# A third buffer for the lower words of the weights, and one weight step moved earlier, in a fused attention and SwiGLU kernel

## The chip, the cores and the metric

One core of one Trainium2 chip runs the whole program. The metric is the device time of one execution in microseconds (us), as a median of several runs. An engine here is one of TensorE (PE), VectorE (DVE), ScalarE (ACT) and GpSimd (POOL); SyncE (SP) issues most of the transfers. PEld is the loading of weights into TensorE, which runs beside its matmuls.

## The reference, cut to what matters

```
scores = (q @ k.T) / sqrt(64)                      # 8 batches x 8 heads, 576 x 576
scores = where(scores >= rowmax(scores) - tau, scores, -1e9)
attn   = softmax(scores)                           # over the kept scores
x      = (attn @ v) as (8*576, 8*64)               # 4608 x 512, heads side by side
g, val = x @ w_gate, x @ w_val                     # 512 -> 1536
out    = (g * sigmoid(g) * val) @ w_out            # 1536 -> 512
```

The inputs of the program are float32, but for the weights (`w_gate`, `w_val`, `w_out`), which come as float64. The kernel itself has to make float32 words of them.

## The kernel before, in words

**Segments and slots.** The attention of two heads of one batch is a segment, `i` = 0 to 31. The main loop (from L864) runs over a list of segments `n`, and within each over its tiles of 128 query rows; one turn of the loop is called slot (n, x) here. Tile 4 is the half tile that holds the last 64 rows. Segments n = 0 to 3 are the first part: tiles 0 and 1 of the four head pairs of batch 0. Segments n = 4 to 7 are the second part: tiles 2, 3 and 4 of the same head pairs. So the first tile of the second part is slot (4,0). From n = 8 on ("halved" in the code) a segment has five tiles.

**A slot.** The order on each engine is the order in which the program issues. A slot issues, in this order: the score matmuls (`sc`, L343, L351 or L356) into two tiles of PSUM, which the slot before has to have left; the row maxima on DVE (L378, L366); the product with `v` of an earlier tile (`xa`, L483, and the ACT copy L489); the threshold and the exponential on ACT (`th` L384 or L381, L385); the turning of the tile before it by PE (`tp`, `end`, L455 to L462) and the ACT copies of that (L463, L467, L468); then a weight step's split and fetch; then the masked product and row sum on DVE (L389), the reciprocal (L414), and the scaling by it on ACT (L397) and POOL (L395); then a join; and then `fill`, which issues a share of the matmuls of the feed-forward block (`pg`, `pv`, L545, with the gate's ACT instructions L558 and L559 and the DVE product L565; later `po`). How much each `fill` issues is set by counts when the program is built, not by time. `xa`, `tp`, `end`, `pg`, `pv` and `po` share four PSUM banks in turn.

**Weight steps.** The weights come in 24 steps of 128 x 768 float64 numbers: steps 1 to 16 for `w_gate` and `w_val`, 17 to 24 for `w_out`. A step is

- a fetch (`fetch_weights`, SP, L182 or L185) into one of six places,
- a split (`split_weights`, ACT): L196 writes the upper words' magnitude into the final place of the weights, and L197 writes a correction from the lower words into a buffer `lo`, taken in turn from the list `los` (L157),
- a join (`join_weights`, DVE and POOL): DVE's L203, L207 and L210 make the float32 bits, and POOL's L212 adds the correction out of `lo`. The place is free for another fetch after L210, and the buffer after L212.

Each slot after the first one splits one step, fetches what it can and joins the oldest that was split. `los` has two buffers, so L197 of step p waits for L212 of step p-2. In two slots, (4,2) and (5,2), which have only the half tile (`double`, L897), two steps are joined at once and a further one is split after them:

```
            double = t == NT and NP <= n < NP + 2
            if more and not double:
                join_weights()
            fill(part)
            next(go)
            fill(part)
            if double:
                join_weights(2)
                split_weights()
                fetch_weights(2)
            gates()
```

`need` keeps the matmuls of the block behind the weights that they read. With this, step 7 is joined in slot (4,0), steps 9 and 10 in (4,2), 13 and 14 in (5,2), 21 in (8,0), 22 in (8,1), 23 in (8,2) and 24 in (8,4). The tile `ob` (pool `op`, one buffer) is where finished output rows are put together; the first of them is written at 249.1 us.

## Time and profile before

| | us |
|---|---|
| median of 5 runs | 1510.97 (1510.58 to 1511.27) |
| the profiled execution | 1511.27, of which its span 1509.5 |
| PE busy in the span | 1483.4 (98%) |
| DVE, ACT, POOL busy | 995.8, 726.5, 642.0 |
| granted PE clock, mean over the span | 0.999 |

The 24 weight steps lie between 17 and 184 us. Busy time is what the profile counts; matmuls overlap, so that one 128x256 matmul stands there with 0.38 us, while a row of 16 in the last part of the trace takes 3.45 us. "Idle before" at an instruction is the time for which its engine had nothing to do ahead of it, and the name after the arrow is what ended this wait.

### The profile page before, as it was taken

To read this page: it belongs to the slowest core of one execution; us is meant where nothing else is said; L and a number is where in the kernel's file an instruction comes from. 1 tells how busy PE (TensorE), PEld (TensorE's weight loads), DVE (VectorE), ACT (ScalarE), POOL (GpSimd) and SP (SyncE) were. 2 spreads that over 40 slices of the span, in tenths; PEclk is the share of its full clock that TensorE was granted. 3 is DMA by queue.
4 is the path that set the end of the run, shared out by engine and by line. 5 is a ranking of instruction groups with operands and counts; after the bars stand their busy time and mean duration, and the time that the engine had idled before them with its cause. 6 is when DMAs were issued, how large, how long until landed. Compare 5 with 4: busy or idle time off the path is not lost. (4 is left out here: it accounts for less than half of the span.)

```text
span 1509.5 us, 31512 instructions
## 1 busy us (share of the span) xinstructions
PE 1483.4 (98%) x11808; PEld 1124.7 (75%) x11808; DVE 995.8 (66%) x3040; ACT 726.5 (48%) x2158; POOL 642.0 (43%) x640
## 2 busy tenths in 40 slices
PE   9999799999999999999999999999999999999998
PEld 6777564477777777787777777777777777888887
DVE  7887987777777777747677666677666767412212
ACT  6777665555545545434545445454544554311110
POOL 2554643366453545435444444544545353500000
PEclk9999999999999999999999999999999999999999
DMA  8643311211112111112111011112110120000000
GB/s 183 178 129 112 76 33 40 53 33 33 46 33 47 33 42 23 40 23 46 33 40 20 21 46 33 46 33 47 33 42 13 40 48 16 1 14 1 15 15 15
DMA packets 177064, 66.93 MB, mean 44 GB/s; under 512 B 159888, under 2 KB 159888, under 8 KB 176912
## 3 DMA queue, kind: packets, MB, share of 16 engines
q1 hardware_dynamic: 170880, 56.62, 16.5%
q0 software_dynamic: 2432, 7.87, 1.4%
q8 instruction: 94, 1.54, 0.4%
q10 hardware_dynamic: 3600, 0.43, 0.2%
q14 instruction: 58, 0.48, 0.1%
HBM read 55.44 MB, written 9.44 MB: 43 GB/s over the span
## 5 line engine op out<-in xcount | busy, mean ns | idle before, releaser
L395 POOL TENSOR_SCALAR pall<-pall,ri 128x288 f32<-128x288 f32 (+1 forms) x260 | 265.0, 1029 | 344.3 <-DVE ri L405 315.1
L545 PE MATMUL pv<-xall,wgv 128*128 128x256 f32 x1728 | 404.0, 382 | 2.4 <-ACT pall L463 2.0
L545 PE MATMUL pg<-xall,wgv 128*128 128x256 f32 x1728 | 403.4, 382 | 0.2 <-ACT pall L463 0.2
L545 PEld LDWEIGHTS pv<-xall,wgv 128*128 128x128 f32 x1728 | 323.6, 190 | 67.7 <-issue 21.8
L545 PEld LDWEIGHTS pg<-xall,wgv 128*128 128x128 f32 x1728 | 323.7, 190 | 65.5 <-issue 22.0
L366 DVE TENSOR_REDUCE mx<-sc 128x2 f32<-128x576 f32 x252 | 180.6, 751 | 237.5 <-PE sc L343 236.7
L389 DVE SCALAR_TENSOR_TENSOR pall<-sc,th,pall 128x288 f32<-128x288 f32 (+1 forms) x540 | 258.2, 528 | 31.4 <-ACT pall L385 31.4
L385 ACT ACTIVATE pall<-sc,nm 128x288 f32<-128x288 f32 (+1 forms) x540 | 236.4, 510 | 0.6
L381 ACT ACTIVATE th<-nm,cut 128x4 f32<-128x4 f32 (+1 forms) x140 | 41.6, 297 | 383.6 <-DVE nm L370 383.6
L577 POOL TENSOR_TENSOR ht<-ht,gt 128x512 f32<-128x512 f32 x84 | 107.0, 1273 | 193.7 <-DVE ht L565 109.8
L434 DVE STREAM_TRANSPOSE pall<-pall 128x576 f32<-128x576 f32 x252 | 181.4, 754 | 2.8 <-POOL pall L395 2.8
L643 PE MATMUL po<-wo,ht 128*128 128x256 f32 x768 | 177.5, 381 | 0.0
L343 PE MATMUL sc<-kT,qT 64*32 64x288 f32 x4032 | 157.8, 410 | 12.8 <-DVE pall L389 11.4
L643 PEld LDWEIGHTS po<-wo,ht 128*128 128x128 f32 x768 | 144.6, 190 | 26.4 <-issue 6.0
L565 DVE SCALAR_TENSOR_TENSOR ht<-tn,pv 128x512 f32<-128x512 f32 x102 | 69.9, 685 | 132.3 <-PE pv L545 119.1
L397 ACT ACTIVATE pall<-pall,ri 128x288 f32<-128x288 f32 (+1 forms) x264 | 132.9, 553 | 0.0
L319 ACT COPY sums<-sums 32x4 f32<-32x4 f32 (+1 forms) x560 | 108.4, 194 | 50.0 <-DVE pall L389 38.6
L558 ACT ACTIVATE tn<-pg 128x512 f32<-128x512 f32 x108 | 64.8, 600 | 139.8 <-PE pg L545 133.0
L509 PE MATMUL xa<-pall,vall 64*64 64x288 f32 x2016 | 128.7, 405 | 0.0
L343 PEld LDWEIGHTS sc<-kT,qT 64*32 64x32 f32 x4032 | 58.7, 105 | 90.4 <-issue 61.6
L509 PEld LDWEIGHTS xa<-pall,vall 64*64 64x64 f32 x2016 | 74.3, 133 | 50.7 <-ACT sums L319 3.6
L661 POOL TENSOR_TENSOR ht<-ht,xall 128x256 f32<-128x256 f32 x48 | 34.1, 729 | 156.3 <-PE po L643 155.1
(110 smaller groups left out, 1338.4 us busy)
## 6 DMA issues: line engine op xcount, KB each, us to landing
vall<-in_v_dram SPq DMA_DIRECT2D x112, 144.0 KB, 3.3
kraw<-in_k_dram SPq DMA_DIRECT2D x114, 72.0 KB, 2.8
qraw<-in_q_dram SPq DMA_DIRECT2D x112, 72.0 KB, 2.4
out_dram<-ob POOLq DMA_DIRECT2D x28, 256.0 KB, 2.8
wo<-in_moe_w_gate_dram SPq DMA_DIRECT2D x16, 384.0 KB, 3.6
wo<-in_moe_w_val_dram SPq DMA_DIRECT2D x16, 384.0 KB, 4.1
xall<-in_moe_w_out_dram SPq DMA_DIRECT2D x5, 768.0 KB, 4.7
wo<-in_moe_w_out_dram SPq DMA_DIRECT2D x3, 768.0 KB, 4.8
```

Source lines behind the costliest of these rows:

```text
L319: nc.scalar.copy(out, in_[:, :, 0])
L343: nc.tensor.matmul(ps[g * G:(g + 1) * G, h, 0:SH], qT[hs, col + a * G:col + (a + 1) * G], kT[hs, c * SH:(c + 1) * SH], start=True, stop=True)
L366: nc.vector.tensor_reduce(out=mx[:, 2 * x:2 * x + 2, 0], in_=tile_[:, :, 0:SH], axis=AX.X, op=ALU.max, negate=True)
L385: nc.scalar.activation(ps[x], scs[x], AF.Exp, bias=nm[:, x:x + 1])
L389: nc.vector.scalar_tensor_tensor(out=ps[x], in0=scs[x], scalar=th[:, x:x + 1], in1=ps[x], op0=ALU.is_ge, op1=ALU.mult, accum_out=sm[:, x, ...
L395: nc.gpsimd.tensor_scalar(out=ps[x], in0=ps[x], scalar1=ri[:, x:x + 1], scalar2=None, op0=ALU.mult)
L397: nc.scalar.activation(ps[x], ps[x], AF.Copy, scale=ri[:, x:x + 1])
L434: nc.vector.transpose(out=p, in_=p)
L509: nc.tensor.matmul(xa[a][h * D:(h + 1) * D, at:at + n * G].rearrange("d (i q) -> d i q", q=G), vr[rs, h, j, :], p[rs, lo:lo + n, j, :], st ...
L545: nc.tensor.matmul(ps[:, i], wgv[:, mat, c, (f + i) * P:(f + i + 1) * P], x[:, c, cs], start=(c == 0), stop=(c == NCC - 1))
L577: eng.tensor_tensor(out=hts[x], in0=hts[x], in1=gt, op=ALU.mult)
L643: nc.tensor.matmul(ps, h(f), w[:, f, :], start=(f == 0), stop=(f == NF2 - 1))
```

## The change

The list `los` gets a third buffer: the memory of `ob`, which no output uses yet while the weights come. And in the slot (4,0), behind its two `fill` calls, one step more is joined, split and fetched.

```diff
@@ in the setup of the weight steps
     los = deque(extra[:, NF * TC + n * TW:NF * TC + (n + 1) * TW] for n in range(2))
+
+    los.append(op.tile([P, 2, DM], F32, name="ob").rearrange("p i n -> p (i n)")[:, 0:TW])
@@ in the main loop
                 join_weights(2)
                 split_weights()
                 fetch_weights(2)
+            elif n == NP and x == 0:
+
+                join_weights()
+                split_weights()
+                fetch_weights(2)
             gates()
```

No instruction is added or taken away on the whole. L197 of step p now waits for L212 of step p-3. From slot (4,0) on every step comes one place earlier in the row: steps 7 and 8 are joined in (4,0), 10 and 11 in (4,2), 14 and 15 in (5,2), 22 in (8,0), 23 in (8,1) and 24 in (8,3). The joins in (8,2) and (8,4) and the splits in (8,1) and (8,3) fall away, and there is a split in (8,2) and a join in (8,3). PE's order of instructions is the same in both kernels.

## The prediction

> **What bounds the kernel now.** I read the page first.

> ```profile
> PE 1483.4 (98%) x11808; PEld 1124.7 (75%) x11808; DVE 995.8 (66%) x3040; ACT 726.5 (48%) x2158; POOL 642.0 (43%) x640
> PE po L643 5%; PE pg L545 4%; PE pv L545 4%; PE xa L509 0%; POOL ht L577 0%; DVE ob L649 0%; POOLq L577 0%
> ```

> PE is busy for 98% of the span, and the chain that ended last is PE work. PE's order of instructions stays the same, and PE takes them in order. So the end moves by the sum of PE's stalls that go or come, and by what PE does at a lower clock. The waits of PE (us in total, times, longest) come next:

> ```profile
> PE sc L343 <- DVE pall L389: 11.4, 12, 2.6
> PE sc L351 <- DVE pall L389: 2.5, 3, 1.3
> PE pv L545 <- ACT pall L463: 2.0, 2, 1.4
> ```

> The two first are scores that wait until DVE has left their PSUM tile. The change touches ACT: the answer for line L197 shows what ACT waited for there.

> ```profile
> its engine sat idle before it (us, times) until:
>   POOL wgv L212: 4.4, 2
> ```

> These are the two double slots, where the third split needs the buffer of a join whose POOL part has just begun. The timeline of ACT and PE at the second of them, slot (5,2) into (6,1):

> ```profile
> 102.48 0.97 ACT L196 ACTIVATE wgv<-wo 128x768 f32<-128x768 f32 x1
> 105.05 1.01 ACT L197 ACTIVATE extra<-wo,minus 128x768 f32<-128x768 uint32 x1 [1.60 <-POOL wgv L212]
> ...
> 106.10 0.31 ACT L384 ACTIVATE th<-nm,cut 128x1 f32<-128x1 f32 x1
> ...
> 108.05 2.13 PE L351 MATMUL sc<-pall 64*128 64x288 f32 x10 [1.32 <-DVE pall L389]
> ```

> ACT waits, the threshold is late, so DVE's L389 is late, so PE stalls. And behind it, by the stretches of the trace (stretch, length, PE busy, granted clock, DMA):

> ```profile
> 109.00:110.00 1.00, 1.00 (x8) 1.00 0.22 82
> 110.00:111.00 1.00, 1.00 (x18) 0.68 0.00 0
> 111.00:112.00 1.00, 1.00 (x9) 0.50 0.00 0
> 112.00:113.00 1.00, 1.00 (x7) 0.50 0.63 53
> 113.00:114.00 1.00, 1.00 (x5) 0.62 0.69 199
> ```

> For some 3.4 us the clock is at half, the only place behind the start where I found it lower: 0.32 + 0.50 + 0.50 + 0.38 = 1.7 us of PE time are lost.

> **The change part by part**, in times of this execution.

> *Slot (4,0), added.* Step 8's join follows step 7's on DVE, which then has a transpose (L912, 62.20) and is idle for 2.99 us until the next maxima (L378, 65.69). L203 waits for step 8's L196 (ends 62.41) and runs beside POOL's L212, where such a row takes 1.00 us (92.92) and not 0.54. So 62.45, then steps of 1.04, 0.98 and 0.88: L912 at 65.35, L378 at 65.8. ACT's added split (0.95 + 1.0 us behind L397, which ends at 63.97) is over at 65.9, before the threshold at 66.48. POOL's L212 (1.8 us) is over at 67.3, before 69.64. SP waits for L210 until 65.4 and its next fetch is at 72.0, so nothing queues there. Cost: 0.1 us; uncovered, the DVE chain would cost 2.5 us.

> *Double slot (4,2).* L197 of step 12 needs L212 of step 9, long done. It runs at 79.5, not at 82.40, so that `xa` is copied at 81.0, and the threshold is bound by L378 and comes at 81.85, not 83.46. PE's 0.32 us before `pv` at 83.61 goes. L389 ends at 84.35, so the next scores (85.53, which took 1.93 us, as their second half waited, against 1.36 elsewhere) save 0.57; 0.29 before `tp` at 89.21 goes. Then L463 is the late one: L378 of (5,1) follows the join at 87.55 (88.83 before), L463 at 90.0, `pg` at 90.6 against 91.88. Gain 1.3 us.

> *Double slot (5,2).* DVE and ACT come 1.7 us earlier into it. L196 of step 16 at 101.0, L197 at 101.85 without a wait, threshold at 103.0 (106.10), L389 at 104.0 (107.08). PE gets to the scores of (6,1) at 105.35, after its second L389 has nearly ended: no stall. Against 108.05 that is 2.7 us in all.

> *Behind it.* Without the half clock slot (6,1) takes PE less: the like slot (7,1) takes 137.63 - 130.47 - 0.57 (stall) = 6.6 us against 116.69 - 108.05 = 8.6. But DVE and ACT do not follow: L378 of (6,1) stands behind a join and L565, at 109.5; L378 of (6,2), 6.15 us later (118.31 - 112.09 = 6.2 before), at 115.65; L463 at 117.25, and `pv` waits for it as at 68.74, until 117.9. Before, it began at 120.94. So of the 2.0 us of clock 1.5 to 1.7 turn into new waits (0.6 for L397 before `tp`, 0.9 for L463), and the gain at this point is 3.0.

> *The fetch of step 17.* Its place is step 14's, so it can only be issued after (5,2)'s join, at 100.9 in the new order, and its split is now one slot later, not two. The rows give 4.8 us to landing: 105.7. ACT wants L196 at 105.25. A wait of 0.5, up to 1.3 with the 6.3 us of its neighbour in that stretch, moves L397 and `tp`, but not L463, which waits for DVE. I take 0.

> *The tail, (8,1) to (9,1).* DVE is without idle from 156.74 to 191.8, and its joins sit ahead of L366 there.

> ```profile
> 166.13 0.72 PE L343 MATMUL sc<-kT,qT 64*32 64x288 f32 x16 [2.60 <-DVE pall L389]
> 173.75 0.72 PE L343 MATMUL sc<-kT,qT 64*32 64x288 f32 x16 [1.50 <-DVE pall L389]
> 180.54 0.72 PE L343 MATMUL sc<-kT,qT 64*32 64x288 f32 x16 [1.34 <-DVE pall L389]
> 187.26 0.72 PE L343 MATMUL sc<-kT,qT 64*32 64x288 f32 x16 [1.48 <-DVE pall L389]
> ```

> A join is 0.56 + 0.56 + 0.96 = 2.1 us. Without (8,2)'s at 166.78, L366 ends 1.7 us earlier, but ACT's split now there pushes the copies L319 from 166.90 to 168.3, so that L404 starts at 169.2, 1.0 earlier: 173.75 becomes 172.8. The join new in (8,3) delays all behind it by 2.1: 180.54 becomes 181.6, so PE stands idle for 3.4 us there. Without (8,4)'s join L366 is then 0.5 early, and PE's own 5.24 us of work to 187.26 - 1.48 set the next scores: 181.6 + 5.24 = 186.85. Net gain 0.4.

> Sum: 3.0 + 0.4 - 0.1 = 3.3 us. On the profiled execution, 1511.27 to 1508.0; it is 0.3 above the median, which gives 1507.7. A difference of 0.2% (3.0 us, so 1507.95) is about what a measurement of this kernel can tell from no change; I stand just beyond it.

> **The rivals.**

> *A second half clock.* The gap of 3.4 us at 178.2 to 181.6 may bring the clock down. For it: 1.32 us of idle time, with narrow matmuls behind, stood ahead of the dip at 110.4. Against it: 2.60 us at 163.5 brought none. The price is the row's 1.7 us, and PE has no slack left for it behind (9,0): gain 1.6, 1509.4. [...]

> *The waits stay away.* If L397 and L463 of (6,1) and (6,2) don't hold PE, the 1.5 us of clock are kept: 1506.2. The steady 6.2 us from one L378 to the next speaks against it.

> *Step 17 late: slower.* One fetch decides it: ACT stands at L196 of step 17 in slot (6,0), and L397, the copy L489 and the threshold of (6,1) are queued behind it. ACT is needed again at about 110.2. If the data land after that, each us costs one; the 3.0 us gained are gone at about 113.2, and the kernel is slower by more than 0.2% from a landing beyond 116, 15 us after the issue. SP's queue is then the cause, as a wait of 13.3 us for a join stands in its answer. At 117: 1514.8. The landing rows of 4.8 and 6.3 us speak against it.

> *It doesn't do what it says.* If the third buffer leaves L197 waiting (for POOL's order, not the buffer), the time is that of before, 1510.9, with 0.1 to 0.3 either way.

> **How the numbers follow.** The sum as it stands: 0.57, of it 0.45 beyond the bound, 0.12 within. The waits stay away: 0.12. Second half clock: 0.18. No effect: 0.05. Step 17 late: 0.08. Faster 0.45 + 0.12 = 0.57; same 0.12 + 0.18 + 0.05 = 0.35; slower 0.08. The range reaches below to 1505.8 (the case at 1506.2 and the 0.4 by which a chain like this can miss) and above to 1510.0 (the half clock, 0.5 of unhidden join in (4,0), and 0.1); it leaves out the two last cases, and some 0.05 of the others.

> **What would show it right or wrong.** Right: no wait of ACT for POOL at L197; scores of (6,1) at about 105.4 with no stall; clock at 1.00 around 107 to 111; `pv` of (6,2) with a wait for L463 at about 117.9; the gap before (9,0)'s second scores at 3 us or more, and none before (9,1). Wrong: an ACT wait for a DMA above 2 us in (6,0); a clock below 1 near 179; L378 of (4,1) more than 0.5 us late.

## The result and the profile after

The changed kernel takes 1508.9 us (median of 27 runs, 1507.39 to 1513.29) against 1510.87 for the kernel before (47 runs). The ratio is 0.9985, with a 95% interval of 0.9979 to 0.999. The forecast was 1507.7, with a range of 1505.8 to 1510.0. The profiled execution took 1509.35 us; its span is 1507.6 and its mean granted clock 0.998.

The times do not scatter about their median but lie in groups: 13 of the 27 at 1507.39 to 1507.84, where the forecast put them, 6 at 1508.9 to 1509.59, 7 at 1510.26 to 1510.59, and one at 1513.29. The profiled execution belongs to the second group. The kernel before has slower executions too, 9 of 47 at 1512.03 to 1514.19, and none of these was profiled. What makes the groups is the main question of the experiments.

In the changed kernel the lines named here have numbers that are 2 higher: L199 is the former L197, L205 the former L203, L214 the former L212, L380 the former L378, L391, L465 and L547 the former L389, L463 and L545. First PE's busy time on the page, then PE's waits (us in total, times, longest):

```profile
PE 1483.7 (98%) x11808; PEld 1124.8 (75%) x11808; DVE 998.0 (66%) x3040; ACT 726.6 (48%) x2158; POOL 641.8 (43%) x640
```

```profile
PE sc L345 <- DVE pall L391: 9.5, 10, 2.6
PE pv L547 <- ACT pall L465: 3.1, 3, 2.3
...
PE sc L353 <- DVE pall L391: 1.2, 2, 0.8
```

PE's work is the same. Its waits for scores fell from 11.4 and 2.5 us to 9.5 and 1.2; the wait of `pv` for L465 rose from 2.0 to 3.1, and its longest one from 1.4 to 2.3. The answer for ACT's line L199, where the kernel before had 4.4 us for POOL in the first list:

```profile
L199 ACT ACTIVATE ob<-wo,minus x6: 996/1040/1082, 23.8 to 109.3; 128x768 f32<-128x768 uint32 x6
...
its engine sat idle before it (us, times) until:
who waited for it (us, times):
  POOL wo L214: 3.2, 1
```

The list of L199's waits is empty: it no longer waits for POOL, and `ob` is in use as the third buffer. The timeline at the second double slot, (5,2) into (6,1), shows the same lines as before:

```profile
103.25 0.93 ACT L198 ACTIVATE wgv<-wo 128x768 f32<-128x768 f32 x1
104.08 0.99 ACT L199 ACTIVATE extra<-wo,minus 128x768 f32<-128x768 uint32 x1
...
105.12 0.29 ACT L386 ACTIVATE th<-nm,cut 128x1 f32<-128x1 f32 x1
```

```profile
107.89 1.36 PE L353 MATMUL sc<-pall 64*128 64x288 f32 x10
...
111.02 1.09 PE L457 MATMUL tp<-pall 128*128 128x128 f32 x8 [0.90 <-ACT pall L399]
...
119.55 2.64 PE L547 MATMUL pv<-xall,wgv 128*128 128x256 f32 x11 [0.22 <-ACT pall L465]
```

From L198 to the threshold it now takes 1.87 us (105.12 - 103.25), and took 3.62 (106.10 - 102.48). The scores of (6,1) start without a stall. Yet they start at 107.89, nearly as late as before (108.05). The stretches of the trace tell why (length, PE busy, granted clock, DMA):

```profile
70.00:71.00 1.00, 1.00 (x5) 0.69 0.47 187
71.00:72.00 1.00, 1.00 (x4) 0.50 0.01 3
72.00:73.00 1.00, 1.00 (x4) 0.50 0.00 0
73.00:74.00 1.00, 1.00 (x4) 0.61 0.26 22
...
109.00:110.00 1.00, 1.00 (x23) 1.00 1.06 410
110.00:111.00 1.00, 0.13 (x4) 1.00 1.04 399
111.00:112.00 1.00, 0.98 (x9) 1.00 1.05 387
```

The half clock at 110 is gone, and another one has come at 70.4 to 73.8 us, right behind the added step. A further one lies in the tail, from 165.9 to 169.4; the last section shows its rows. The tail, in PE's timeline:

```profile
164.73 0.72 PE L345 MATMUL sc<-kT,qT 64*32 64x288 f32 x16 [2.60 <-DVE pall L391]
...
172.41 0.72 PE L345 MATMUL sc<-kT,qT 64*32 64x288 f32 x16
...
180.16 0.72 PE L345 MATMUL sc<-kT,qT 64*32 64x288 f32 x16 [2.31 <-DVE pall L391]
...
185.33 1.54 PE L345 MATMUL sc<-kT,qT 64*32 64x288 f32 x32
```

The stalls of 1.50 and 1.48 are gone, and the one in slot (9,0) has grown from 1.34 to 2.31.

### The profile page after: what moved, and what is told of

Read it like the earlier page. It is cut to its first block, busy times and chain, and to the rows that moved or that the text cites. A ratio compares the mean times of both kernels' runs of the same rounds, so it can differ in the third digit from the quotient of the medians.

```text
span 1507.6 us, 31516 instructions
## 1 busy us (share of the span) xinstructions
PE 1483.7 (98%) x11808; PEld 1124.8 (75%) x11808; DVE 998.0 (66%) x3040; ACT 726.6 (48%) x2158; POOL 641.8 (43%) x640
## 5 line engine op out<-in xcount | busy, mean ns | idle before, releaser
L397 POOL TENSOR_SCALAR pall<-pall,ri 128x288 f32<-128x288 f32 (+1 forms) x260 | 265.4, 1030 | 344.0 <-DVE ri L407 323.5
L547 PE MATMUL pv<-xall,wgv 128*128 128x256 f32 x1728 | 407.0, 384 | 3.1 <-ACT pall L465 3.1
L547 PE MATMUL pg<-xall,wgv 128*128 128x256 f32 x1728 | 403.2, 382 | 0.7 <-ACT pall L465 0.7
L547 PEld LDWEIGHTS pv<-xall,wgv 128*128 128x128 f32 x1728 | 325.9, 191 | 69.2 <-issue 22.1
L547 PEld LDWEIGHTS pg<-xall,wgv 128*128 128x128 f32 x1728 | 323.5, 190 | 66.0 <-issue 22.0
L391 DVE SCALAR_TENSOR_TENSOR pall<-sc,th,pall 128x288 f32<-128x288 f32 (+1 forms) x540 | 258.1, 528 | 27.6 <-ACT pall L387 27.6
L579 POOL TENSOR_TENSOR ht<-ht,gt 128x512 f32<-128x512 f32 x84 | 107.0, 1273 | 191.7 <-DVE ht L567 107.4
```

The lines of the kernel that those rows point to most:

```text
L391: nc.vector.scalar_tensor_tensor(out=ps[x], in0=scs[x], scalar=th[:, x:x + 1], in1=ps[x], op0=ALU.is_ge, op1=ALU.mult, accum_out=sm[:, x, ...
L397: nc.gpsimd.tensor_scalar(out=ps[x], in0=ps[x], scalar1=ri[:, x:x + 1], scalar2=None, op0=ALU.mult)
L547: nc.tensor.matmul(ps[:, i], wgv[:, mat, c, (f + i) * P:(f + i + 1) * P], x[:, c, cs], start=(c == 0), stop=(c == NCC - 1))
L579: eng.tensor_tensor(out=hts[x], in0=hts[x], in1=gt, op=ALU.mult)
```

## The experiments

The same point of the trace lies up to 1.3 us apart in two executions even ahead of the change, so points are compared here by their distance from the first `xa` of 14 products in slot (4,0), at 59.81 before, 59.90 after.

**The changed kernel again, unaltered.** No edit.

> The changed kernel once more, unaltered. Theory (the time steps by stretches of half clock of 3.4 us, 1.7 us of PE each, whose place differs between executions): times in groups near 1507.6, 1509.2 and 1510.4, the slower groups with the lower mean clock (0.999, 0.998 to 0.997, 0.996); this profile has its stretches of half clock at other places than 70 and 166 us, or another number of them, and PE waits that agree with those of the first profile to 0.1 us elsewhere. Rival (the places are fixed by the kernel): the profile again shows 70.4 to 73.8 and 166 to 169.4, and the times form one group near 1509.

1508.12 us, median of 10 (1507.29 to 1510.06), ratio 0.998 [0.9971, 0.9989]. Five times lie at 1507.29 to 1507.56, four at 1508.68 to 1509.27, one at 1510.06. The profiled one took 1507.36, and its clock is whole at 70 to 74. So here is an execution of the first group to set beside that of the second:

| us from the first `xa` to | before | changed, 1509.35 | changed, 1507.36 | buffer alone |
|---|---|---|---|---|
| `pv` of (4,1) | 8.93 | 9.81 | 9.81 | 8.93 |
| scores of (6,1) | 48.24 | 47.99 | 46.32 | 45.72 |
| `pv` of (6,2) | 61.13 | 59.65 | 58.01 | 57.88 |
| scores of (9,3) | 143.36 | 141.34 | 139.70 | 140.12 |

The two executions of one kernel are alike up to `pv` of (4,1). From there the one with the half clock is later by 1.64 us, and stays so to the end (141.34 - 139.70). The rows of this `pv`, with PE's wait ahead of it, in the kernel before, in the execution of 1509.35 and in that of 1507.36:

```profile
68.74 2.86 PE L545 MATMUL pv<-xall,wgv 128*128 128x256 f32 x12 [1.40 <-ACT pall L463]
...
69.71 4.54 PE L547 MATMUL pv<-xall,wgv 128*128 128x256 f32 x12 [2.27 <-ACT pall L465]
...
69.37 2.86 PE L547 MATMUL pv<-xall,wgv 128*128 128x256 f32 x12 [2.27 <-ACT pall L465]
```

Both executions of the changed kernel wait 2.27 us there; in one of them the same products then take 4.54 us and in the other 2.86.

**The third buffer alone.**

```diff
-            elif n == NP and x == 0:
-                join_weights()
-                split_weights()
-                fetch_weights(2)
```

> The third buffer alone, without the step added in slot (4,0). Theory (the buffer carries the gain, the added step costs 0.9 in slot (4,1) and gives back 0.5 in the tail): no wait of ACT for POOL at the lower words; PE's wait before pv in (4,1) 1.4 us as before the change; scores of (6,1) without a stall; waits of 1.5, 1.3 and 1.5 us in the tail as before the change; fastest group of times near 1507.1 to 1507.4, and fewer slow executions than with the added step, as the gap in (4,1) is shorter. Rival 1 (the buffer saves only the stalls, and the half clock at 110 us stays): 1508.8. Rival 2 (the step added is what counts): 1510.5 or more.

1507.93 us, median of 10, ratio 0.9977 [0.9967, 0.9986]. Nine of the ten lie at 1507.82 to 1508.03, some 0.5 us above what was expected, and one at 1508.79. The buffer alone has the whole gain up to `pv` of (6,2), 61.13 - 57.88 = 3.25 us, keeps it to the end (143.36 - 140.12 = 3.24), and has no groups. By the medians it is 1.0 us faster than with the step added.

**The added step alone**, with two buffers.

```diff
-    los.append(op.tile([P, 2, DM], F32, name="ob").rearrange("p i n -> p (i n)")[:, 0:TW])
```

> The step added in slot (4,0) alone, with two buffers. Theory: ACT's waits for POOL in the two double slots are back (2.8 and 1.6 us), the scores of (6,1) stall by 1.3 us, PE's wait before pv in (4,1) is 2.3 us; tail 0.5 better than before; 1511.3 without a further stretch of half clock, 1513 with one. Rival (the added step is the gain): 1509 or less.

1511.88 us, median of 11 (1510.17 to 1513.29), ratio 1.0003 [0.9994, 1.0011]: nothing by itself, and a wide spread. In its profile (1511.88; 1513 was expected with such a stretch) `pv` of (4,1) waits 2.28 us and a half clock follows at 69.6 to 73.0.

**Steps 7 and 8 joined as a pair**, behind the two fills of (4,0), as the double slots do it.

```diff
-            double = t == NT and NP <= n < NP + 2
+            double = t == NT and NP <= n < NP + 2 or n == NP and x == 0
...
-            elif n == NP and x == 0:
-                join_weights()
-                split_weights()
-                fetch_weights(2)
```

> Both parts, but in slot (4,0) the two steps 7 and 8 are joined as one pair behind the two fills, as in the double slots, so that DVE does both steps' L203 and L207 before step 7's last DVE instruction lets POOL begin. ACT's and POOL's order is that of the changed kernel. Theory (step 8's first DVE row took 2.23 us as POOL's L212 had started 0.01 us before it and held it until POOL's end): both rows take 0.54 to 0.6 us, the maxima of (4,1) come at 65.8 and not 66.7, PE's wait before pv in (4,1) is 1.5 and not 2.3 us, fastest group near 1506.7. Rival (a join more costs its length there, whatever POOL does): wait 2.2 us or more, 1507.6 as in the changed kernel.

1507.78 us, median of 7 (1506.85 to 1508.33), ratio 0.9973 [0.9962, 0.9984]. DVE's and POOL's timelines show what the pair changes. The changed kernel:

```profile
62.52 1.82 POOL L214 TENSOR_TENSOR wgv<-wgv,extra 128x768 uint32<-128x768 uint32 x1 [0.57 <-ACT wgv L198]
62.53 2.23 DVE L205 TENSOR_SCALAR wgv<-wgv 128x768 f32<-128x768 f32 x1 [0.16 <-ACT wgv L198]
...
66.69 1.38 DVE L380 TENSOR_REDUCE nm<-sc 128x1 f32<-128x576 f32 x2
```

The pair:

```profile
62.48 0.56 DVE L205 TENSOR_SCALAR wgv<-wgv 128x768 f32<-128x768 f32 x1 [2.17 <-ACT wgv L198]
...
65.00 2.40 POOL L214 TENSOR_TENSOR wgv<-wgv,extra 128x768 uint32<-128x768 uint32 x1 [3.10 <-DVE wgv L212]
...
66.06 1.39 DVE L380 TENSOR_REDUCE nm<-sc 128x1 f32<-128x576 f32 x2
```

L205 started 0.01 us behind POOL's addition of step 7 and took 2.23 us, over POOL's end at 64.34. Where POOL's addition comes later, L205 takes 0.56. `pv` of (4,1) then waits 1.69 us instead of 2.27. Three of the seven times lie at 1506.85 to 1507.03.

**The gap of (4,1) filled.** PE's one transpose into `end` ahead of that `pv` is issued 16 times.

```diff
-                    nc.tensor.transpose(end[:, 0:P], both, unit)
+                    for _ in range(16 if seg is segs[NP] and t == TA else 1):
+                        nc.tensor.transpose(end[:, 0:P], both, unit)
```

> The changed kernel with the gap of PE before pv of slot (4,1) filled: the one transpose into `end` there is issued 16 times instead of once, with the same values (15 x about 0.12 us = 1.75 us of work). Theory: the executions above 1508.5 us are those in which the clock falls to half behind the 2.27 us wait of pv in (4,1). With the gap filled no half clock comes at 70 to 74 us; nearly all times lie at 1507.2 to 1507.8, the median near 1507.5. Rival: the groups come from somewhere else in the execution (a dip behind the gap of 2.3 us in (9,0)); the times stay spread as in the unaltered kernel, half of them at 1508.7 to 1510.4.

1508.72 us, median of 11, ratio 0.9981 [0.9972, 0.999]. Half of the theory fell: 3 times lie at 1507.44 to 1507.71, but 8 at 1508.64 to 1509.02, where nearly none was expected. Half held: none lies above 1509.02, and the profile (1509.02) has no half clock at 70. It has one at 178.7 to 182.2, behind a wait of 3.24 us in (9,0):

```profile
163.07 0.72 PE L345 MATMUL sc<-kT,qT 64*32 64x288 f32 x16 [2.60 <-DVE pall L391]
...
169.68 0.72 PE L345 MATMUL sc<-kT,qT 64*32 64x288 f32 x16 [0.50 <-DVE pall L391]
...
178.53 1.08 PE L345 MATMUL sc<-kT,qT 64*32 64x288 f32 x16 [3.24 <-DVE pall L391]
```

So there are two places, and this run tells them apart.

**The added step two segments later**: none in (4,0), and (6,2) a third double slot.

```diff
-            double = t == NT and NP <= n < NP + 2
+            double = t == NT and NP <= n < NP + 3
...
-            elif n == NP and x == 0:
-                join_weights()
-                split_weights()
-                fetch_weights(2)
```

> The third buffer with the added step in another place: none in (4,0), and slot (6,2) a third double slot, so that two steps are joined behind its two fills. Theory: PE waits 1.4 us before pv of (4,1), as in the kernel before, so there is no half clock there; the join in (6,2) lies beside work of PE and costs 0 to 0.3; the tail is that of the changed kernel (joins in (8,0), (8,1) and (8,3), some 0.5 us gained). About 1507.3, without the group at 1509. Rival: the join of 2.1 us in (6,2) is in the chain DVE maxima, threshold, L389, pall that holds PE in (7,0), and costs its 2.1 us whole: 1509.5.

1508.09 us, median of 10, ratio 0.9977 [0.9968, 0.9986]. Five times lie at 1507.37 to 1507.55, as expected; five at 1508.64 to 1509.09, which the theory did not have. The join in (6,2) costs nothing (1507.4, as the first group of the changed kernel). The profile is of the second group, and its clock falls in (9,0):

```profile
177.00:178.00 1.00, 0.00 (x0) 1.00 0.62 97
178.00:179.00 1.00, 0.70 (x16) 0.55 0.74 116
179.00:180.00 1.00, 1.00 (x13) 0.50 0.60 95
180.00:181.00 1.00, 1.00 (x4) 0.50 1.12 186
181.00:182.00 1.00, 1.00 (x5) 0.74 0.93 279
```

From these scores to those of (9,3) it takes 22.24 us (178.30 to 200.54), and 21.08 in the execution of 1507.36 (178.18 to 199.26). The half clock in (9,0) thus costs 1.16 us here (1.30 by the same points in the profile with the gap of (4,1) filled, 178.53 to 200.91), and that in (4,1) 1.64. From the first group at 1507.6, one of them makes 1508.8 or 1509.2, and both make 1510.4: the groups of the changed kernel.

**Two more profiles of the changed kernel.**

> The changed kernel once more, for a further profile. Theory: if its time is above 1508.5, the profile shows a half clock at about 70 to 74 us (as the first profile), and above 1510 a third stretch of half clock behind another gap of more than 2 us; if it is below 1507.8, none at 70. Rival: a slower execution without any further half clock.

> As the run before it: a further profile of the changed kernel, with the same expectations (above 1508.5: half clock at 70 to 74 us; below 1507.8: none there).

1509.33 and 1509.03 us. Both have the half clock behind `pv`'s wait in (4,1), of 2.29 and 2.27 us, as the first profile has. None above 1510 was caught, so that both half clocks make the third group rests on the sum above and on the runs with a gap filled: with that of (4,1) filled none of 11 times is above 1509.02.

**Both gaps filled.** Besides the transposes in (4,1), five products of 128 x 256 ahead of the first scores of (9,0), into a tile that the scores overwrite.

```diff
+            for _ in range(5 if seg is segs[2 * NP + 1] and t == tiles[0] else 0):
+                nc.tensor.matmul(pss[0][:, 0, 0:256], kT[:, 0:P], kT[:, 0:256], start=True, stop=True)
```

> The changed kernel with both gaps of PE filled: 16 transposes in place of one ahead of pv in (4,1), and 5 matmuls of 128x256 (2.26 us, into a tile that the scores then overwrite) ahead of the first scores of (9,0), so that the wait of 2.3 us ahead of its second scores is taken up. Theory: the changed kernel's times come in three groups, about 1507.4 (no half clock that counts), 1508.7 to 1509.3 (one, at 70 or at 179 us) and 1510.4 (both). With both gaps filled all times lie at 1507.2 to 1507.8. Rival: half clock comes from the narrow scores beside the gaps, or from other places, and a group at 1508.7 stays.

1507.67 us, median of 10, ratio 0.9974 [0.9965, 0.9984]. Nine of the ten lie at 1507.58 to 1507.81, one at 1508.41. The groups are gone, and the profile's mean granted clock is whole:

```profile
core 0: 1505.9 us, clock 1.000
```

The kernel does 4 us more of PE work and is 1.2 us faster than the changed one by the medians, which is the clearest sign that its groups come from PE's clock behind these two gaps.

**Only the gap of (9,0) filled.**

> The changed kernel with the gap ahead of the second scores of (9,0) filled alone (5 matmuls of 128x256). Theory: the gap in (4,1) stays and brings its half clock in some of the executions: two groups, 1507.4 and 1509.0 to 1509.4, none at 1510.4. Rival: the group above 1510 has nothing to do with (9,0) and stays.

1509.24 us, median of 11, ratio 0.9982 [0.9973, 0.9991]. Three times lie at 1507.48 to 1507.67 and six at 1509.16 to 1509.37, as expected. One at 1510.5 was not expected and has no profile, so this run by itself does not rule out its rival. The profiled one (1508.58) has a half clock neither in (4,1) nor in (9,0); it has one at 7.8 to 11.2 us, in the first scores, and its first `xa` is 0.96 us later than with both gaps filled. So there are further places, hit less often.

**The pair, with the gap of (9,0) filled**: the two edits shown above.

> Steps 7 and 8 joined as a pair in (4,0), with the third buffer, and the gap of (9,0) filled as in the two runs before it. Theory: the pair alone had groups at 1506.9 and at 1507.8 to 1508.3; the second group is the half clock behind the gap of (9,0), so with it filled all times lie at 1506.7 to 1507.2, the fastest kernel of this study. Rival: the second group has another source (the half clock at 163.5) and stays: median 1507.7.

1507.1 us, median of 7, ratio 0.9975 [0.9964, 0.9986]. Four lie at 1506.96 to 1507.1, the others at 1508.12, 1508.17 and 1509.31, so the theory that all would be in the first group failed. The profiled one (1508.12) has its half clock at 43.7 to 47.1, in the first part. By the medians it is the fastest kernel here, 1.8 us below the changed kernel and 0.8 below the buffer alone; its interval overlaps with those of the buffer alone and of both gaps filled, so that which of the three is fastest is not shown.

**The half clock at 110 by itself.** The kernel before, with PE's gap ahead of the scores of (6,1) filled by more products into `end` in (6,0). ACT's waits stay.

```diff
-                for hs in (slice(0, D), slice(D, P)):
+                for hs in (slice(0, D), slice(D, P)) * (6 if seg is segs[NP + 1] else 1):
```

> The kernel before, with its gap of 1.32 us ahead of the scores of (6,1) filled by repeating the four 64x64 products into `end` in (6,0) (10 more, 1.3 us); ACT's two waits for POOL stay. It measures the half clock at 110 us by itself. By the prediction's step, 1.5 to 1.7 of the 1.7 us of PE time turn into new waits for L397 and L463, as DVE's and ACT's chain sets pv of (6,2): no clock below 1 at 107 to 114, pv of (6,2) with a wait of 0.6 or more, the time 0 to 0.4 us below that of before (about 1510.6). Rival: the half clock is the main part of the gain; then the time falls by 1.5 us, to 1509.4.

1510.95 us, median of 11, ratio 0.9997 [0.9988, 1.0005]. The ten products took 0.55 us instead of the expected 1.3, and a wait of 0.71 us ahead of the scores of (6,1) is left. But the clock is whole there in this profile, and the time is that of before:

```profile
110.00:111.00 1.00, 1.00 (x20) 1.00 0.00 0
111.00:112.00 1.00, 1.00 (x13) 1.00 0.00 0
```

```profile
120.79 0.92 PE L545 MATMUL pv<-xall,wgv 128*128 128x256 f32 x3 [0.72 <-ACT pall L463]
```

`pv` of (6,2) waits 0.72 us for L463 where it waited for nothing before. Its distance is 60.68 (120.79 - 60.11), 0.45 less than before. Of the 1.7 us that the half clock takes from PE, 0.45 are worth anything by these two executions, and by the medians nothing. How often the kernel before has this half clock is not known, as there is one profile of it.

## Why the prediction was right or wrong, point by point

**The sum.** The gain was put at 3.3 us and measured at 2.0 (1510.87 to 1508.9); the time lies within the range. The forecast of 1507.7 describes the first group, half of the executions (18 of 37 in the two sets). That the median is in the range as well is owed to the upper end, which was set for a half clock in another place. The 1.3 us that are missing come from one term that was too small, the added join, and from a rival that was held too unlikely; both follow below.

**The double slots, right.** The buffer alone moves the scores of (6,1) by 48.24 - 45.72 = 2.52 us; 2.7 was predicted. They start without a wait, though there the second half of them is late (1.80 us instead of 1.36).

**The clock that turns into waits, right.** Predicted for `pv` of (6,2): 3.0 us earlier, held by L463. Measured: 3.25 with the buffer alone, 3.12 in the execution of 1507.36, both with a wait for L465 (0.70 and 0.73). The run on the half clock alone agrees. The rival in which the waits stay away is out.

**Step 17's fetch, right.** ACT waits 1.01 us for it at 108.45, 0.34 in the execution of 1507.36. `tp` is late by it (0.90 in the profile shown), `pv` of (6,2) is not.

**The added join in (4,0), wrong: this is the step that failed.** The prediction gave L203 1.00 us from the row at 92.92, "beside POOL's L212". That row's neighbour is another one:

```profile
92.77 1.72 POOL L395 TENSOR_SCALAR pall<-pall,ri 128x576 f32<-128x576 f32 x1 [1.89 <-DVE ri L414]
92.92 1.00 DVE L203 TENSOR_SCALAR wgv<-wgv 128x768 f32<-128x768 f32 x1 [0.25 <-issue]
```

It is the scaling L395, with one tensor as input, not the addition L212 with two. Beside the addition the same instruction took 2.23 us. L380 started at 66.69 (66.60 as the profile before counts) and not at 65.8. The prediction had named a delay of it above 0.5 us as a sign of being wrong. `pv` of (4,1) is 0.88 us late, not 0.1. POOL's instruction was first in both cases, by 0.01 us beside the addition and by 0.15 us beside the scaling; why the first took 2.23 us and the second 1.00 was not shown.

By itself the error is small: the wait for L465 in (6,2) takes back all but 0.13 of the 0.88 (3.25 against 3.12). But it made PE's gap in (4,1) 2.27 us instead of 1.40, and behind this gap the half clock came in about half of the executions (with the gap of (9,0) filled, 6 of 11 times lie in its group). Together with the half clock of (9,0) that moved the median from the 1507.6 of the first group to 1508.9: with only the gap of (4,1) filled it is 1508.72, with only that of (9,0) 1509.24, with both 1507.67.

**The rival of a second half clock: right in kind, wrong in place and chance.** It was given 0.18 and put behind the gap of (9,0), with 1.7 us. It does come there, for 1.16 us, and more often in (4,1), for 1.64, where the prediction saw no gap. What failed is the argument against it, "2.60 us at 163.5 brought none". One execution can't show that: of the 14 profiles of this study, that of before among them, 11 have a half clock behind that same gap of 2.60. The half clock behind that gap costs nothing, as PE waits for DVE in (8,4) and (9,0) anyway: from the scores of (8,3) to the second ones of (9,0) it takes 15.41 us with it (162.77 to 178.18 at 1507.36) and 15.46 without (163.07 to 178.53 with the gap of (4,1) filled).

**The tail, right with an exception.** The net gain behind (6,2) was put at 0.4; against the buffer alone, whose tail is that of before, it is 0.55 ((58.01 - 57.88) + (140.12 - 139.70)). (9,1) has no stall, as predicted. The earlier scores of (8,4) and the gap of 3.4 us in (9,0) come true only where the clock is whole at 163 to 167: 0.50 us of wait in (8,4) and 3.24 in (9,0) with the gap of (4,1) filled. Elsewhere the half clock takes PE's gain in (8,4), and the gap in (9,0) is 2.3.

## What to carry to other kernels

A step that was put beside a stall cost here not its own time but what followed from the gap that it made: 0.88 us of delay cost 0.1 at `pv` of (6,2) where the clock stayed whole and 1.8 where it did not (58.01 and 59.65 against 57.88). So after each sum, list PE's gaps of the new order, and take those of the size that half clock followed here in some executions (2.27 to 3.24 us) for a chance of it, whatever one profile shows. A kernel with groups of times is read group by group: one profile of each, and then the gap filled with work of PE whose result nobody uses, which is a cheap proof and here also a gain. And before a row is used as a price, look up what ran beside it, by its line.

## What the runs showed of the hardware that was not expected

**The starts of the half clock fit a grid.** In the profile of the changed kernel it holds from 70.38 to 73.78 and from 165.94 to 169.36 (from the shares of the stretches: 70 to 71 with 0.69 is 0.62 us at half). The first and the last row of the second one:

```profile
165.00:166.00 1.00, 0.84 (x32) 0.97 0.00 0
...
169.00:170.00 1.00, 1.00 (x6) 0.82 0.00 0
```

The two last 3.40 and 3.42 us, and their starts lie 95.56 us apart. That is 28 lengths of 3.413 us; 27 or 29 would make a length of 3.54 or 3.30. The other six profiles with two stretches agree: their starts lie 4, 28 (twice), 29, 35 and 46 times 3.413 us apart, to 0.02 us. The grid does not lie alike in two executions of the changed kernel: the starts at 70.38 and, in the profile of 1509.03, at 69.46 are 2.12 and 1.20 us past a multiple of 3.413. So, if the starts keep to such a grid, how much of a gap falls into one cell of it differs between executions.

**DVE's scaling beside POOL** took different times: 2.23 us beside an addition of two tensors that had begun 0.01 us earlier (62.53 in the profile of the changed kernel), 1.00 us beside a scaling that had begun 0.15 us earlier (92.92 before), 0.54 alone (22.87 in the profile of the changed kernel). In other rows L205 took 1.09 us beside the product of two tensors L579, begun 0.60 us earlier, and ended 0.41 us behind it (87.34 in the profile of the changed kernel), and the same instruction took 0.54 beside POOL's L254, a scaling too, begun 0.37 us earlier (29.61 before). What makes the difference was not tried.

**What stays open**: why the pair in (4,0) gains 0.5 us more than the single step by the first groups (1506.9 against 1507.4), the two half clocks behind little idle time (at 110 before and at 43.7 with the pair), the slower executions of the kernel before, and the single times above all groups (1513.29 of the changed kernel, 1510.5 with the gap of (9,0) filled).
